# RWKV-7 recurrence with a SoLU block: decayed state made at the end of a chunk, weights narrowed in more stages, another order in the first slots

## The chip, the cores and the metric

The kernel runs on one core of one Trainium2 chip. The metric is the device time of one launch in microseconds (us), as a median over runs. The kernel before takes 893.51 us (three runs, 891.63 to 895.63). Its profiled execution has a span of 898.0 us. Times with a place in the span, such as "at 561 us", count from the start of that profiled span.

The core has five engines that work side by side, each through its own list of instructions in order: TensorE (PE; its weight loads are listed as PEld), VectorE (DVE), ScalarE (ACT), GpSimd (POOL) and SyncE (SP). SP only issues transfers here. An instruction that waits holds up all that stand behind it on its engine.

## The reference, cut to what matters

```python
for t in range(S):                       # S = 768, B = 4, H = 8, D = 40
    y[:, :, t] = einsum('bhd,bhde->bhe', rt, state)
    Sa = einsum('bhde,bhe->bhd', state, at)
    state = state * wt[:, :, None, :] - einsum('bhd,bhe->bhde', Sa, bt) + einsum('bhd,bhe->bhde', vt, kt)
x = y.transpose(0, 2, 1, 3).reshape(B * S, H * D)        # 3072 x 320
h = x @ w_in                                             # 320 x 1024
e = exp(h - max(h));  solu = h * e / (sum(e) + 1e-9)
ln = (solu - mean(solu)) / sqrt(var(solu) + 1e-6) * g_ln
out = ln @ w_out                                         # 1024 x 320
```

Thirty-two recurrences (4 batches of 8 heads), each with a 40 x 40 state, feed a row-wise block. The inputs of the recurrence are float32; `w_in`, `w_out` and `g_ln` as handed over are 64-bit or 32-bit floats, and the 64-bit weights are made into float32 on the chip.

## The kernel before, in words

Time is cut into 12 chunks (rounds) of 64 steps. A round has two **slots**, one for each half of the recurrences, so there are 24 slots, `i = 0..23`. Within a chunk the recurrence is a triangular system: its matrix is inverted once per round, and the state is carried from chunk to chunk by matmuls.

The pieces of work are Python generators, and an order written out by hand decides how they interleave on each engine:

- `front(i)` (letters f, g) makes the decayed keys of slot `i`, up to the score matrix `nt` (L276). It runs five slots ahead (`AHEAD`).
- `scatter(n)` writes the 32 x 32 blocks of `nt` of round `n` to DRAM (`blk_dram`, L385) and `gather(n)` reads them back with one matrix per partition (`blk`, L392). `gather` can be issued only when the scatter has landed.
- `invert(n)` (letter I) inverts those blocks on DVE: one start step (L400 to L404), 30 steps of a product (L410) and a subtraction (L412), and one last step that transposes (L415) and writes both forms to DRAM (L418, L420). That is 32 steps.
- `bring_inverse(i)` reads the inverse of slot `i` back in eight transfers (`tinv` L431, `tinvT` L434), and `solve(i)` (letter s) joins the blocks to 64 x 64.
- `attend(i)` (letter a) prepares what doesn't depend on the state.
- `recurrence(i)` (letter r) has six steps: the product with the state (`px` L520, added to `x` on DVE, L522); its transpose (`psT`); `pu` and its copy `nuT` on ACT (L541, L546); `plamu` and its copy `lamu` on DVE (L274, L276); `pnu`; and `pst` with the new state (L567, `tot` L573, `st` L574). `readout(i)` (letter y) makes `pyo` and the DVE copy `x` (L587, L594).
- `weights()` (letter W) fetches the weights in 26 pieces, ten of `w_in` and sixteen of `w_out` (L213), and narrows each one: DVE takes the exponent and mantissa apart (L163, L166), ACT converts them (L165, L168, L169), DVE puts the sign back (L171), POOL adds and multiplies (L173, L174). At its end the mean of the weights is taken out (L236, L238).
- `hidden(i)`, its later steps, and `output(i)` (letters h, b, o) are the row-wise block. It runs six slots behind the recurrence (`LAG`).

Ahead of slot 0 stands a prologue (fronts 0 to 3, the inverse of round 0 and eleven steps of that of round 1). Slots 0 to 5 follow the list `EARLY` and carry the weights; slots 6 to 23 follow `STEADY` and carry the row-wise block; the last six row blocks have no recurrence beside them (the tail). The lists are

```python
EARLY = ("r r f I W r a r r I W y r a f I W a s a f W a f s f W a f", ...)
STEADY = "r r f b b I r o o a o r r I o y o r I o a f h a s a h f I a h f s h f h a f h h"
```

Each `I` takes four steps. In an odd slot the first of them is the start of a new inverse, and `steps(inv, 99)` (L742) ends it at the close of the next even slot. The gather of that inverse is issued at the head of the same odd slot (L727), in the SP queue behind the scatter that the slot before issued last (L744).

Two-deep pools matter too: PSUM tiles of one bank (`bank`, two of them), of two banks (`duo`, two of them) are handed out in turn, so a copy out of PSUM that is late holds up the matmul two allocations on.

Of the kernel before, what the change touches and what calls it, by code (L numbers as in the profile page):

```python
# [9 lines left out]
FP32 = mybir.dt.float32  # L10
# [7 lines left out]
P = 128  # L18
Q = 32
# [33 lines left out]
def kernel(  # L53
# [86 lines left out]
    sm_t = zeroed(nc.vector, "sm", [P, 2, G, 64], 1)  # L140
    st_t = [const.tile([P, 2, G, D], FP32, name=f"st{i}") for i in range(2)]
# [14 lines left out]
    def narrow(dst, land, tmp):  # L156
# [8 lines left out]
        nc.scalar.activation(out=scale, in_=scale, func=AF.Relu, scale=2.0 ** 23, bias=ebias[0:n])  # L165
        nc.vector.tensor_scalar(out=man, in0=hi, scalar1=0xFFFFF, scalar2=None, op0=ALU.bitwise_and)  # L166
        frac, rest = man.bitcast(FP32), low.bitcast(FP32)
        nc.scalar.activation(out=frac, in_=man, func=AF.Copy, scale=2.0 ** -20, bias=1.0)  # L168
# [3 lines left out]
                                       op1=ALU.bitwise_or)  # L172
        nc.gpsimd.tensor_tensor(out=frac, in0=frac, in1=rest, op=ALU.add)  # L173
# [3 lines left out]
    def weights():  # L177
# [4 lines left out]
        pg = bank("pg")  # L182
        nc.tensor.transpose(out=pg[:, 0:NF], in_=g_rows, identity=ident[0:NF, 0:NF])
        nc.scalar.copy(out=g_col, in_=pg[:, 0:NF])
# [31 lines left out]
        for j in range(3):  # L216
            fetch(j)
        yield
        open_ = None
        for j, (dst, _) in enumerate(pieces):  # L220
            new = None
            if not exact:
                new = narrow(dst, land[j % 4], temps[j % 2])
            for part in (new, open_):
                if part:
                    next(part)
            open_ = new
            fetch(j + 3)
            yield
        if open_:  # L230
            next(open_)
# [78 lines left out]
    def decay(i):  # L310
# [6 lines left out]
            ax[:, :, at:at + 2].rearrange("q g c -> q c g").unsqueeze(3).to_broadcast([P, 2, G, D])  # L317
            for at in (2 * P, 2 * P + 2)]
# [6 lines left out]
        for j, n in ((1, "b"), (0, "k")):  # L325
            nc.gpsimd.tensor_tensor(out=keyed(kb[:, j])[:, :, :, 0:D], in0=by_heads(given(i, n)),  # L326
                                    in1=inv.rearrange("q (g p d) -> q p g d", p=2, d=D), op=ALU.mult)
        yield
        lo = where["cum_ex"][0]
# [17 lines left out]
    def front(i):  # L347
# [3 lines left out]
        copy = nc.scalar.copy if i < 2 else nc.gpsimd.tensor_copy  # L351
        parts = decay(i)
        next(parts)
        if i >= 2:
            copy(out=keyed(a)[:, :, :, 0:D], in_=by_heads(given(i, "a")))
# [5 lines left out]
        if i < 2:  # L361
            copy(out=keyed(a)[:, :, :, 0:D], in_=by_heads(given(i, "a")))
# [31 lines left out]
    def invert(n):  # L394
# [7 lines left out]
        nc.vector.memset(u[half(1)], 0.0)  # L402
        for p in range(2):
            nc.vector.memset(u[half(p)].rearrange("b c t -> b (c t)")[:, p:Q * Q // 2:Q + 2], 1.0)  # L404
        yield
        for j in range(1, Q - 1):
# [6 lines left out]
            yield  # L413
        ut = two.tile([P, Q, Q // 2], FP32, tag="ut", name="ut", bufs=1)
        nc.vector.tensor_copy(out=ut, in_=u.rearrange("p c t -> p t c"))  # L415
        ut_dram = of_round[n]["ut"] = dram.tile([P, Q, Q // 2], FP32, tag="ut_dram", name="ut_dram")
        u_dram = of_round[n]["u"] = dram.tile([64, Q, Q], FP32, tag="u_dram", name="u_dram")
        nc.sync.dma_start(out=ut_dram, in_=ut)  # L418
        for p in range(2):
            nc.sync.dma_start(out=u_dram.rearrange("b (c z) t -> b c z t", z=2)[:, :, p], in_=u[half(p)])  # L420
        yield

    def bring_inverse(i):
# [5 lines left out]
        for q in (0, 2):  # L429
            for p in range(2):  # L430
                nc.sync.dma_start(out=tinv[quarter(q), :, p],  # L431
                                  in_=ut[half(p)][homes(q, s)].rearrange("h s t -> s h t"))
# [75 lines left out]
    def recurrence(i):  # L508
        d = st[i]
        ci, s = divmod(i, 2)  # L510
        state, sm, nu = st_t[s], sm_t[0], nu_t[0]
        kb, vb = d["kb"], given(i, "v")
        x0 = x0_t[i % 2]
        if ci:
            nc.gpsimd.tensor_tensor(out=sm[:, :, :, 0:D], in0=state, in1=d["to_mid"], op=ALU.mult)
# [45 lines left out]
        if ci < NCH - 1:  # L561
# [9 lines left out]
            if ci:  # L571
                tot = two.tile([P, 2, G, D], FP32, tag="tot", name="tot", bufs=1)
                nc.vector.tensor_tensor(out=tot, in0=new, in1=sm[:, :, :, 0:D], op=ALU.add)  # L573
                nc.gpsimd.tensor_tensor(out=state, in0=tot, in1=d["to_end"], op=ALU.mult)  # L574
            else:
                nc.vector.tensor_tensor(out=state, in0=new, in1=d["to_end"], op=ALU.mult)
# [103 lines left out]
    def turns(order, more, **parts):  # L680

        for x in order.split():
            steps(parts.get(x), more.get(x, 1))

    def fronts(i):
# [3 lines left out]
    EARLY = ("r r f I W r a r r I W y r a f I W a s a f W a f s f W a f",  # L689
             "r r f g I W r a r r I W y r a f g I W a s a f g W a f g s f g W a f g")  # L690
    STEADY = "r r f b b I r o o a o r r I o y o r I o a f h a s a h f I a h f s h f h a f h h"
# [8 lines left out]

    with tc.manual_schedule():
        load(0, "w", "b", "a", "k")
        load(1, "w", "b")
        f, g = front(0), front(1)
        turns("f f g g f f g g f f g g f g", {}, f=f, g=g)
        scatter(0)
        load(1, "a", "k")
        gather(0)
        inv = invert(0)
        load(0, "v", "r")  # L710
        f, g, at = front(2), front(3), attend(0)
        turns("I I f f g g f f g g I f g f g I f I g a a a", dict(I=3), f=f, g=g, I=inv, a=at)
        scatter(1)
        gather(1)
        load(2, "w", "a")
        steps(inv, 99)
        bring_inverse(0)
        load(1, "v", "r")
        load(2, "b", "k")
        inv, so = invert(1), solve(0)  # L720
        turns("a a I s a I s", dict(I=4), a=at, s=so, I=inv)
        begin(0)
        ws, after, before = weights(), None, None
        for i in range(N):
            m, more, js = i - LAG, i + 1 < N, fronts(i)
            if i % 2 and (i + 3) // 2 < NCH:
                gather((i + 3) // 2)  # L727
                inv = invert((i + 3) // 2)
# [55 lines left out]
```

## Time and profile before

| stretch of the span | what runs | length, us |
|---|---|---|
| 0 to 82.9 | prologue, up to the `pu` of slot 0 | 82.9 |
| 82.9 to 302.5 | slots 0 to 5 (`pu` of slot 0 to `pu` of slot 6) | 219.6 |
| 302.5 to 361.7 | slots 6 and 7 | 59.2 |
| 361.7 to 671.0 | slots 8 to 18 | 309.3 |
| 671.0 to 773.0 | slots 19 to 22, up to the last `pu` | 102.0 |
| 773.0 to 898.0 | slot 23 and the tail | 125.0 |

Over the whole span PE is busy for 663.6 us (74%), DVE for 464.2 (52%), ACT for 272.1 (30%), POOL for 127.1 (14%). The stretches above are cut at the first `pu` matmul (L541) of a slot, since there is one per slot and it stands on the path from state to state. In the page's part 2, each digit is the busy share of a fortieth of the span (22.45 us) in tenths; PEclk is the granted TensorE clock in the same slices. In the timeline a bracket gives the idle time of the engine just before an instruction, and who ended it.

### The profile page before, as it was taken

What the parts mean: (1) busy time and instruction counts of PE and PEld (TensorE: products, weight loads), DVE (VectorE), ACT (ScalarE), POOL (GpSimd) and SP (SyncE); (2) the same over time, 40 slices, a digit from 0 to 9 for tenths busy, and PEclk for the clock granted to TensorE, in tenths of its full rate; (3) what the DMA queues carried; (4) which work ended last, traced back from release to release, by engine and by line L of the source; (5) the groups of instructions that cost most, each with busy time, mean ns of one, the idle gap of its engine ahead of it and who ended that gap; (6) DMA issues with size and microseconds to landing.
All of it is one profiled execution on the core that took longest, in us unless ns stands there. A gap on an engine that the chain in (4) does not pass through costs nothing.

```text
span 898.0 us, 28194 instructions
## 1 busy us (share of the span) xinstructions
PE 663.6 (74%) x12281; PEld 464.5 (52%) x12281; DVE 464.2 (52%) x1257; ACT 272.1 (30%) x633; POOL 127.1 (14%) x202
## 2 busy tenths in 40 slices
PE   6423726537537878989989899897988888878786
PEld 4312525426435646656656666565665665534444
DVE  2651646446443756657667675674765633222231
ACT  4110415314312332334423344233432333211111
POOL 2101304213111100111101111011100000000000
PEclk9655758657656998999999999999999999887978
DMA  6577133533533332635345453352324211000000
GB/s 111 88 129 135 38 80 84 109 76 70 100 75 55 63 64 56 97 55 95 73 82 95 74 101 77 57 104 52 58 52 79 49 28 31 8 19 7 16 15 15
DMA packets 269803, 60.01 MB, mean 67 GB/s; under 512 B 255464, under 2 KB 265328, under 8 KB 269680
## 3 DMA queue, kind: packets, MB, share of 16 engines
q1 hardware_dynamic: 269536, 57.98, 34.5%
q8 instruction: 97, 1.59, 0.8%
q10 hardware_dynamic: 144, 0.23, 0.1%
q14 instruction: 26, 0.21, 0.1%
HBM read 40.08 MB, written 13.37 MB: 60 GB/s over the span
## 4 chain that ended last, share of the span: by engine, by line
PE 51%; DVE 16%; SPq 10%; DMA 9%; ACT 7%; issue 6%; POOL 0%; ACTq 0%; DVEq 0%; POOLq 0%
PE h L615 13%; PE po L660 10%; DMA blk<-blk_dram 4%; SPq L300 4%; DVE u L412 3%; DVE prod L410 3%; PE pyo L587 3%; PE pcx L333 3%; DVE nmax L625 2%; PE pst L567 2%; DMA blk_dram<-nt 2%; SPq L385 2%; ACT e L629 2%; DVE e L632 2%; PE plnT L655 2%
## 5 line engine op out<-in xcount | busy, mean ns | idle before, releaser
L615 PE MATMUL h<-w_in,xT 128*128 128x512 f32 (+1 forms) x288 | 137.1, 682 | 19.6 <-DVE e L632 16.5
L660 PE MATMUL po<-w,lnT 128*128 128x320 f32 x384 | 129.0, 471 | 0.1
L412 DVE TENSOR_TENSOR u<-u,prod 128x30 f32<-128x30 f32 (+4 forms) x360 | 109.0, 303 | 12.4
L410 DVE TENSOR_TENSOR prod<-blk,u 128x30 f32<-128x30 f32 (+4 forms) x360 | 98.8, 274 | 10.0
L660 PEld LDWEIGHTS po<-w,lnT 128*128 128x128 f32 x384 | 71.6, 201 | 27.9 <-issue 6.8
L625 DVE TENSOR_REDUCE nmax<-h 128x1 f32<-128x1024 f32 x24 | 29.4, 1225 | 82.4 <-PE h L615 82.4
L615 PEld LDWEIGHTS h<-w_in,xT 128*128 128x128 f32 (+1 forms) x288 | 40.4, 201 | 46.3 <-issue 42.8
L665 ACT ACTIVATE osb<-po,rs 128x320 f32<-128x320 f32 x24 | 12.7, 528 | 164.1 <-PE po L660 124.0
L274 PE MATMUL plamu<-rT,nuT 64*64 64x64 f32 x768 | 18.2, 241 | 48.8 <-ACT nuT L546 48.8
L632 DVE TENSOR_TENSOR e<-h,e 128x1024 f32<-128x1024 f32 x24 | 29.4, 1225 | 44.1 <-ACT e L629 44.1
L326 POOL TENSOR_TENSOR kx<-raw_b,inv 128x320 f32<-128x320 f32 x24 | 21.0, 873 | 219.3 <-ACT inv L324 206.2
L333 PE MATMUL pcx<-cst,lw 128*128 128x132 f32 x192 | 34.6, 313 | 15.3 <-ACT y_mid L490 10.8
L333 PEld LDWEIGHTS pcx<-cst,lw 128*128 128x128 f32 x192 | 29.4, 212 | 27.0 <-ACT y_mid L490 15.9
L276 DVE TENSOR_TENSOR lamu<-plamu,cst 128x512 f32<-128x512 f32 x24 | 16.5, 689 | 50.3 <-PE plamu L274 50.3
L400 DVE TENSOR_SCALAR u<-blk 64x512 f32<-64x512 f32 x12 | 5.2, 431 | 71.9 <-DMA blk<-blk_dram 67.5
L541 PE MATMUL pu<-tinvT,x 64*64 64x64 f32 x768 | 20.2, 246 | 29.8 <-DVE x L522 19.4
L274 PEld LDWEIGHTS plamu<-rT,nuT 64*64 64x64 f32 x768 | 15.6, 153 | 50.0 <-ACT nuT L546 50.0
L647 POOL TENSOR_TENSOR rs<-c,mhalf 128x1 f32<-128x1 f32 x24 | 13.1, 548 | 194.6 <-DVE c L646 180.7
L165 ACT ACTIVATE parts<-parts,ebias 128x160 int32<-128x160 int32 (+1 forms) x26 | 11.9, 458 | 92.6 <-DVE parts L163 92.6
L656 ACT COPY lnT<-plnT 128x512 f32<-128x512 f32 x48 | 26.9, 603 | 41.7 <-PE plnT L655 41.6
L574 POOL TENSOR_TENSOR st<-tot,kx 128x320 f32<-128x320 f32 x20 | 14.8, 738 | 168.7 <-DVE tot L573 168.7
L541 PEld LDWEIGHTS pu<-tinvT,x 64*64 64x64 f32 x768 | 16.8, 150 | 39.9 <-DVE x L522 27.3
(108 smaller groups left out, 1222.4 us busy)
## 6 DMA issues: line engine op xcount, KB each, us to landing
blk<-blk_dram SPq DMA_DIRECT2D x24, 256.0 KB
raw_w<-in_w_dram SPq DMA_DIRECT2D x24, 160.0 KB
raw_b<-in_b_dram SPq DMA_DIRECT2D x24, 160.0 KB
raw_a<-in_a_dram SPq DMA_DIRECT2D x24, 160.0 KB
raw_k<-in_k_dram SPq DMA_DIRECT2D x24, 160.0 KB
v<-in_v_dram SPq DMA_DIRECT2D x24, 160.0 KB
r<-in_r_dram SPq DMA_DIRECT2D x24, 160.0 KB
out_dram<-osb SPq DMA_DIRECT2D x24, 160.0 KB
```

Source lines behind the costliest of these rows:

```text
L274: nc.tensor.matmul(t[half(c ^ p * cross), p, g * L:(g + 1) * L], lhsT=lhs[half(p), g, half(c)], rhs=rhs[half(p), g, half(c)], start=True, ...
L300: nc.sync.dma_start(out=to[half(c)], in_=ap[2 * c:2 * c + 2, :, n * L:(n + 1) * L, :] .rearrange("b h t d -> t (b h) d"))
L333: nc.tensor.matmul(t[:, g * 132:g * 132 + 132], lhsT=pair(lw, 2 * j + g), rhs=cst[:, lo:lo + 132], start=True, stop=True)
L410: nc.vector.tensor_tensor(out=t, in0=nb[:, j:j + 1, j + 1:Q].to_broadcast([P, rows, m]), in1=u[:, 0:rows, j:j + 1].to_broadcast([P, rows, ...
L412: nc.vector.tensor_tensor(out=u[:, 0:rows, j + 1:Q], in0=u[:, 0:rows, j + 1:Q], in1=t, op=ALU.subtract)
L541: nc.tensor.matmul(t[half(z), c ^ p, h // 2 * L:h // 2 * L + L], lhsT=x0[half(c ^ p), h, :], rhs=d["tinvT"][half(c ^ p), p, h % G, :], sta ...
L587: nc.tensor.matmul(t[half(p), c, g * L:g * L + L], lhsT=kb[half(c), j, 2 * g + p, :], rhs=lam[half(c), h % 2, h // 2, :], start=i < 2 and ...
L615: nc.tensor.matmul(h[:, j * 512:j * 512 + 512], lhsT=of_round[i // 2]["xT"][rows, kt, i % 2 * P:i % 2 * P + P], rhs=w_in[rows, 4 if kt == ...
L625: nc.vector.tensor_reduce(out=nmax, in_=h, axis=AX.X, op=ALU.max, negate=True)
L632: nc.vector.tensor_tensor(out=q, in0=h, in1=e, op=ALU.mult)
L656: nc.scalar.copy(out=lnT[:, fs.start:fs.stop].rearrange("p f t -> p (f t)"), in_=t)
L660: nc.tensor.matmul(o[:, 0:DM], lhsT=lnT[:, f, :], rhs=w2[:, f, :], start=f == 0, stop=f == NF - 1)
```

## The change

**Decayed state.** The kernel before ends a chunk with `state = tot * to_end` and begins the next with `sm = state * to_mid`, both on POOL. The changed kernel forms the small factor `fac = to_end * to_mid(next)` (128 x 8) and ends the chunk with `sm = tot * fac`; `sm` is kept for both slots of a round and `st` is dropped.

**Weights in stages.** A piece is narrowed in four steps instead of two: DVE apart, ACT, DVE sign, POOL, each in a half-step `W` of its own; there are ten `W` in a slot in place of five, and pieces are fetched two ahead instead of three. `g_rows` is transposed at the end of the weights, no longer at their start.

**Order of the first slots.** The prologue loads in another order, doesn't interleave the inverse of round 0 (it runs as one block), leaves that of round 1 to slot 0, and brings the first `tinv` by the ACT queue. The `a` copies are all on POOL, and `k` is multiplied a step after `b`.

**Inverses as one stream.** All later inverses are one generator. In `EARLY` and `STEADY` the first `I` of a slot now stands behind `lamu` (the fourth r), not ahead of `pu`. The steps per `I` are `[6, 6, 3, 3]` in an even slot and `[0, 6, 4, 4]` in an odd one, so that a new inverse starts behind the sixth r of an odd slot. Half of the start of an inverse (a memset of 64 x 512 and one of 64 x 16) moves to POOL. `kT` moves ahead of `pu`, the front's `pcum` behind it, and the second half of the `plnT` transposes behind `plamu`; `b` and `k` are loaded in mid-slot.

```diff
-    sm_t = zeroed(nc.vector, "sm", [P, 2, G, 64], 1)
-    st_t = [const.tile([P, 2, G, D], FP32, name=f"st{i}") for i in range(2)]
+    sm_t = zeroed(nc.vector, "sm", [P, 2, G, 64], 2)
...
-        pg = bank("pg")
-        nc.tensor.transpose(out=pg[:, 0:NF], in_=g_rows, identity=ident[0:NF, 0:NF])
-        nc.scalar.copy(out=g_col, in_=pg[:, 0:NF])
...
-            new = None
-            if not exact:
-                new = narrow(dst, land[j % 4], temps[j % 2])
-            for part in (new, open_):
-                if part:
-                    next(part)
+            new = None if exact else narrow(dst, land[j % 4], temps[j % 2])
+            for _ in range(2):
+                for part in (open_, new):
+                    if part:
+                        next(part)
+                if _:
+                    fetch(j + 2)
+                yield
             open_ = new
-            fetch(j + 3)
-            yield
...
-        nc.vector.memset(u[half(1)], 0.0)
-        for p in range(2):
-            nc.vector.memset(u[half(p)].rearrange("b c t -> b (c t)")[:, p:Q * Q // 2:Q + 2], 1.0)
+        nc.gpsimd.memset(u[half(1)], 0.0)
+        for p, engine in enumerate((nc.vector, nc.gpsimd)):
+            engine.memset(u[half(p)].rearrange("b c t -> b (c t)")[:, p:Q * Q // 2:Q + 2], 1.0)
...
+        if ci < NCH - 1:
+            fac = small.tile([P, 2, G], FP32, tag="fac", name="fac")
+            nc.gpsimd.tensor_tensor(out=fac, in0=d["to_end"], in1=st[i + 2]["to_mid"], op=ALU.mult)
+            factor = fac.unsqueeze(3).to_broadcast([P, 2, G, D])
         if ci:
-            nc.gpsimd.tensor_tensor(out=sm[:, :, :, 0:D], in0=state, in1=d["to_mid"], op=ALU.mult)
...
-                nc.gpsimd.tensor_tensor(out=state, in0=tot, in1=d["to_end"], op=ALU.mult)
+                nc.gpsimd.tensor_tensor(out=sm[:, :, :, 0:D], in0=tot, in1=factor, op=ALU.mult)
...
-    EARLY = ("r r f I W r a r r I W y r a f I W a s a f W a f s f W a f",
-             "r r f g I W r a r r I W y r a f g I W a s a f g W a f g s f g W a f g")
-    STEADY = "r r f b b I r o o a o r r I o y o r I o a f h a s a h f I a h f s h f h a f h h"
+    EARLY = ("r r a r f r W I r W y W r I W W a f L a s W a f W a W I f I W s f W a f",
+             "r r a r f g r W I r W y W r I W W a f g L a s W a f g W a W I f g I W s f g W a f g")
+    STEADY = "r r b b a r f o r o I o r o y o r I o a f L h a s a h f a I h f I s h f h a f h h"
...
+    def inverse_steps(i):
+        if i < 3:
+            return [[6, 6, 6, 6], [0, 3, 4, 3], [6, 6, 5, 5]][i]
+        return [0, 6, 4, 4] if i % 2 else [6, 6, 3, 3]
...
-        load(1, "w", "b")
...
-        inv = invert(0)
         load(0, "v", "r")
-        f, g, at = front(2), front(3), attend(0)
-        turns("I I f f g g f f g g I f g f g I f I g a a a", dict(I=3), f=f, g=g, I=inv, a=at)
+        load(1, "k")
+        f, g, at, inv, so = front(2), front(3), attend(0), invert(0), solve(0)
+        turns("f g f g f f g g", {}, f=f, g=g)
+        load(2, "w", "a", "b", "k")
+        turns("a a I", dict(I=99), a=at, I=inv)
+        bring_inverse(0, nc.scalar)
+        turns("a a a f g f g a f g", {}, f=f, g=g, a=at)
         scatter(1)
         gather(1)
...
             if i % 2 and (i + 3) // 2 < NCH:
                 gather((i + 3) // 2)
-                inv = invert((i + 3) // 2)
+            if i == 1:
+                steps(inv, 8)
...
             if i % 2 == 0:
-                load((i + 6) // 2, "w", "a", "b", "k")
-            turns(EARLY[len(js) - 1] if i < LAG else STEADY, dict(I=4), **parts)
+                load((i + 6) // 2, "w", "a")
+                parts["L"] = later((i + 6) // 2)
+            turns(EARLY[len(js) - 1] if i < LAG else STEADY, dict(I=inverse_steps(i)), **parts)
...
-            else:
-                steps(inv, 99)
```

## The prediction

> **What bounds the kernel now.** I cut the span at the `pu` matmul (L541) that stands once in each slot: 82.94, 107.48, 148.68, 186.37, 219.67, 256.79, 302.55 us for slots 0 to 6, then 326.84, 361.73, 388.80, 419.48, 445.86, 475.19, 501.56, 529.77, 556.14, 586.53, 612.89, 644.60, 670.98. The view of busy time by stretch comes first (us of the stretch, then busy time of PE, PEld, DVE, ACT, POOL, then the granted clock, the DMA share and GB/s):
>
> ```profile
> 0.00:82.90 82.90, 29.12 (x377) 22.17 (x377) 33.22 (x112) 16.07 (x35) 15.06 (x30) 0.70 0.70 117
> 82.90:302.50 219.60, 125.51 (x2881) 103.26 (x2881) 110.82 (x331) 70.40 (x190) 48.04 (x77) 0.68 0.37 75
> ...
> 361.70:671.00 309.30, 276.76 (x5742) 191.78 (x5742) 200.33 (x533) 111.62 (x252) 44.69 (x65) 0.98 0.42 77
> ```
>
> For 302 us no engine is near full and PE runs at two thirds of its clock: latency bounds. Slots 8 to 18 are PE's, 276.8 of 309.3 us. Next, who waited for whom (us, times, longest):
>
> ```profile
> ACT parts L165 <- DVE parts L163: 92.6, 18, 19.6
> ...
> DVE u L400 <- DMA blk<-blk_dram: 67.5, 11, 10.3
> ...
> PE plamu L274 <- ACT nuT L546: 48.8, 5, 20.4
> ...
> PE pyo L587 <- DVE lamu L276: 22.4, 8, 5.1
> ...
> PE pg L183 <- DMA g_rows<-in_moe_g_ln_dram: 16.7, 1, 16.7
> ```
>
> These are links of one chain, as the timeline of slot 1 shows:
>
> ```profile
> 121.04 1.13 SPq L392 DMA_DIRECT2D blk<-blk_dram  x2
> ...
> 124.65 0.42 DVE L400 TENSOR_SCALAR u<-blk 64x512 f32<-64x512 f32 x1 [9.17 <-DMA blk<-blk_dram]
> ...
> 127.73 0.51 ACT L165 ACTIVATE parts<-parts,ebias 128x256 int32<-128x256 int32 x1 [19.65 <-DVE parts L163]
> ...
> 128.77 0.70 ACT L546 ACTIVATE nuT<-pu 128x256 f32<-128x256 f32 x3
> 129.18 0.94 PEld L274 LDWEIGHTS plamu<-rT,nuT 64*64 64x64 f32 x32 [20.61 <-ACT nuT L546]
> 129.18 1.13 PE L274 MATMUL plamu<-rT,nuT 64*64 64x64 f32 x32 [20.37 <-ACT nuT L546]
> ```
>
> DVE waits for the gather, ACT for DVE's L163 behind it, and `nuT` stands behind that on ACT. Slots 3 and 5 repeat it (10.6 us each). In the late odd slots only DVE's part is left (slot 15):
>
> ```profile
> 561.49 0.42 DVE L400 TENSOR_SCALAR u<-blk 64x512 f32<-64x512 f32 x1 [3.38 <-DMA blk<-blk_dram]
> ...
> 564.17 0.68 DVE L276 TENSOR_TENSOR lamu<-plamu,cst 128x512 f32<-128x512 f32 x1
> ```
> ```profile
> 564.91 0.69 PE L587 MATMUL pyo<-lamu,kx 64*64 64x64 f32 x32 [2.29 <-DVE lamu L276]
> ...
> 566.23 2.35 PE L660 MATMUL po<-w,lnT 128*128 128x320 f32 x4
> ```
>
> The gap in front of `pyo` is followed by `po` at 2.35 us where the even slot before has 1.34: the gap is paid about twice.
>
> **What the skill says.** The Trainium skill's "TensorE: Matmul & The Clock Gate", Part 1, says that the array falls to half rate after an idle window of about 3.4 us and needs as long a busy one to recover. The trace agrees in kind: `plamu` of 32 takes 1.13 us after a stall and 0.65 in a full slot. Its "DMA: Bandwidth & Descriptors", "Anatomy of one DMA", says that [...]waits on semaphores are taken by the issuing sequencer. The trace: the gather is issued 1.9 us behind the scatter's last issue in slots 14 and 15, and SP does nothing else meanwhile. Its "Trainium Kernel Development and Optimization", "Key Constraints", says that another issuing queue saves only issue time. Four `tinv` issues take 1.8 to 2.2 us here, so moving them to ACT is worth no more.
>
> **Part by part.**
>
> *Steady slots.* Even slots last 26.37 us (slots 10 to 18; slot 8 27.07). Odd ones with a gather last 30.68, 29.33, 28.21, 30.39, 31.71 (slots 9 to 17): excess over 26.37 is 4.3, 3.0, 1.8, 4.0, 5.3, sum 18.4. The start of an inverse moves behind `tot`, some 9 us later than now (561.5 against 570.9), when `blk` has been there for 9 us. So the wait goes, and its cold clock. Slot 19 has no front, and lasts 27.3 us where slot 21, with no gather either, takes 25.4: 1.9 more. Slot 7 lasts 34.9 us with a 5.1 us wait for `lamu` and cold matmuls; without them it is like slot 6, 24.3 us: 10. Order on PE: `kT` now fills the gap ahead of `pu` (0.41 + 0.49 us idle, because `x` L522 comes late), `pcum` no longer waits for L319, and `po` no longer for both `lnT`: 0.3 us in each of some 15 slots, 4.5. Added: six inverse steps behind `lamu` of an even slot take 6 x 0.63 = 3.8 us instead of 2.5. `x` L594 stands behind them and `pst` needs the PSUM pair that `x` frees. But `plnT`'s half, `po`, `pnu`, `po`, `pyo`, which lie between, are 5.2 us of PE: hidden. On POOL half the start of an inverse (0.5 us, as the DVE memset) stands behind `sm`; L412 waits for it 1 us, and only `psi` is behind, needed 8 us later. The decayed state: 22 POOL multiplications of 0.74 us go, 22 of 128 x 8 come. `st` was ready at 541.4 and `sm` needed at 553: worth nothing. Sum: 18.4 + 1.9 + 10 + 4.5 = 34.8 us.
>
> *Prologue.* Now `tinvT` is done at 63.0 and `pu` starts at 82.94, since `pg` waits for `g_rows` in front of it. That wait goes. The uninterrupted inverse: 60 operations with gaps, 16.9 us, plus 0.9, from 27 (two loads fewer ahead of the gather, now 28.7) to 45. Then `u` and `ut` issues 1.7, landing 3.5, `tinv` on ACT 2, `rT` 0.6 (it stands behind them on ACT), then PE from `plamv` to `pz` about 9.5, `tinvT` 0.9: `pu` at 63, 20 us earlier.
>
> *Slots 0 to 5.* That gain is not kept, because SP's queue is as long as before. The last `nt` of round 1 comes at about 60. Behind it on SP: scatter 2.3, its landing 1.9, gather 1.1, `v` and `r` 2.8, eight returns 4.0, `w` and `a` 2.8, `g_rows` 0.7: the first weight piece is issued at 75.8 and lands at 79.5 (3.7 us from issue to the DVE that waits for it at 174.78). In slot 0 DVE's L163 for it stands ahead of `x`, and `pst` behind `x`: `pst` at 81 (now 88.8). Then six inverse steps and a piece stand ahead of `vT` (ACT waits for the piece: 7 us), and twelve steps around `paT`: the `pu` of slot 1 comes at 107, as now. Slot 1 loses its 20.4 us stall, but DVE begins with eight steps (4.3 us). The seventh piece is queued on SP behind scatter, gather, the writes of `u` and `ut`, 3.5 us of landing and eight returns: issued at 122, landed at 126, with DVE and ACT waiting from 119. `pu` of slot 2 at 142 (now 148.7): 6.7 us won. Slots 2 and 4: now 37.7 and 37.1, of which 7.5 + 4.5 and 6.5 + 3.9 are waits for pieces and for the ending inverse; the pieces come in time, as `b` and `k` are loaded behind them. But six steps and a piece between `pst` and `vT` cost some 4.5: 30.2 and 31.2, 7.5 and 5.9 won. Slot 3, 33.3, loses 10.6; the gather now holds DVE at `tot` for about 1 us and the piece behind it for 1.5, with three more for steps: 28.2, 5.1 won. Slot 5, 45.8, likewise loses 10.6 and some 2.2 of half-rate matmuls behind the stall: 33, 12.8 won. `mean` itself (7.1 us and 4 us of waiting) stays. Sum 0 + 6.7 + 7.5 + 5.1 + 5.9 + 12.8 = 38.0.
>
> The tail has no change. Total 38.0 + 34.8 = 72.8: 893.5 - 72.8 = 820.7 us.
>
> **Unknown costs, both ends.** How long SP holds a piece back in slots 0 and 1: nothing (all of the prologue's 20 us and the 20.4 us stall won, some 34 more than my 6.7) or another 8 us in each of slots 1, 3, 5. I take the queue as counted, since every issue in it has a row now. How many of the moved steps show on the path in slots 2 to 5: none (3 to 4.5 us less each) or all six plus cold clock (3 us more each).
>
> **The rivals.** *All stalls go, and none takes their place:* slots 0 to 5 then run at the 24.5 us that slot 0 takes now, plus 12 for `mean`: 159 from 63 on, so `pu` of slot 6 at 222, 80 won; with 34.8, 778 us. For it: DVE has 110.8 us to do in 219.6. Against: SP's issues alone, some 40 us per two slots, stand in order with those two landings. Chance 0.10. *The start gives nothing:* the pieces, fetched two ahead instead of three, wait for SP in every slot and take back the 38. Then 859 us. For it: DVE waited 9.7 us twice for pieces fetched three ahead. Chance 0.15. *Slower:* blocks of six steps hold up `x`, `psi`, `paT`'s copy; PE, which is 89% busy in the steady part, goes cold in each slot, 1.3 us of wait paid twice in 17 slots is 44, and the steady gain is eaten; the start loses 20 to piece waits. 893.5 - 34.8 + 44 + 20 = 923 us. Against: DVE is busy for 18.0 of the 26.4 us of slot 14, so 8 us are free. Chance 0.04.
>
> **How the numbers follow.** The forecast has 0.71: 820.7 us. Its own bounds are 800 (half the missed start) and 840 (three slots with 8 us more, less the rest). The range of 796 to 850 takes in these, half of the case in which the start gives nothing and a little of the best. Faster 0.95 (all but the last case and its fringe), the same 0.01, slower 0.04.
>
> **What would show it.** In the changed profile: `pu` of slot 0 near 63 and of slot 6 near 264; no wait of DVE L400 longer than 1 us from slot 7 on; steady odd slots as long as even ones, 26.2 us; PE waits in slots 0 and 1 that end on DVE, behind transfers named `bits`. It would be wrong if `pu` of slot 6 stays near 300, or if steady slots wait for `x` behind inverse steps.

## The result and the profile after

The changed kernel takes 850.08 us (846.64 to 853.63) where the kernel before took 893.31 beside it: ratio 0.9515, interval 0.9466 to 0.9563. The forecast was 820.7 us. So the direction was right, and 43 us came where 73 were forecast; the measured time lies at the upper end of the forecast's range of 796 to 850 us. The profiled pair differs by more, 898.0 against 844.7 us: the profiled run of the changed kernel is the fastest of its four timed ones, and that of the kernel before took longer than all of its timed ones. About 4.5 us of that pair's difference lie behind the last `pu` (at 772.2 us in the kernel before, not at 773.0 as in the table of the time before), in 440 matmuls whose granted clock differed (0.83 against 0.85). The list of the tail is the same in both kernels, and the profiles of the changed kernel and of those variants of it that keep this tail have 121.3 to 124.7 us behind the last `pu`; so most of the 4.5 us can be chance.

The start of `pu` (L544 now), in us, for slots 0 to 8 and 19: 66.70, 116.54, 151.25, 180.45, 209.81, 238.49, 276.08, 297.90, 325.11 and 627.25. Cut there, forecast and measurement stand like this:

| stretch | gain forecast | gain in the profiles |
|---|---|---|
| start to `pu` of slot 0 | 20.0 | 16.2 |
| slot 0 | -20.0 | -25.3 |
| slots 1 to 5 | 38.0 | 35.5 |
| slots 6 and 7 | 10.6 | 10.2 |
| slots 8 to 18 | 21.7 | 7.1 |
| slot 19 to the end | 2.5 | 9.5 |
| sum | 72.8 | 53.2 |

(The forecast's 0.3 us per slot for the order on PE is spread over the slots 6 to 20.) The view of busy time by stretch, of the changed kernel, with the columns as in the prediction:

```profile
66.70:276.10 209.40, 122.40 (x2886) 101.36 (x2885) 116.84 (x352) 72.19 (x192) 53.60 (x90) 0.72 0.47 94
...
325.10:599.90 274.80, 251.10 (x5223) 179.72 (x5223) 175.67 (x476) 102.47 (x230) 39.12 (x70) 0.96 0.44 83
```

The slots 0 to 5 are still latency: PE has no more to do than before and runs at 0.72 of its clock. In the steady slots 8 to 17 the granted clock is 0.96, lower than before, although the long stalls are gone. The list of waits says what took their place:

```profile
PE pu L544 <- DVE x L525: 25.5, 13, 2.7
...
PE pcx L337 <- ACT vT L259: 22.8, 2, 22.1
...
DVE parts L162 <- DMA bits<-in_moe_w_in_dram: 18.2, 2, 11.3
DVE prod L410 <- POOL u L404: 17.5, 8, 8.9
...
DVE u L400 <- DMA blk<-blk_dram: 14.3, 4, 8.1
...
PE py L478 <- DMA bits<-in_moe_w_in_dram: 10.0, 1, 10.0
```

(`pcx`, `paT` and `pbT` belong to a front, `vT` and `psi` to `attend`, `py` and `pz` to `solve`; `plnT` are the transposes of the row-wise block that stand ahead of `po`, its last product.)

DVE's wait for the gather fell from 67.5 us in eleven places to 14.3 in four, and PE no longer waits for `nuT` or `pg`. Two of the new lines are not in the forecast's sum: DVE waits for GpSimd's memset, 8.9 us once, and PE waits for `x` in front of `pu` thirteen times, 1.36 us at the end of even slots and 2.67 at the end of odd ones, where it had waited 0.49. The timeline of the prologue shows the first:

```profile
24.44 0.42 DVE L400 TENSOR_SCALAR u<-blk 64x512 f32<-64x512 f32 x1 [8.06 <-DMA blk<-blk_dram]
...
25.90 2.02 SPq L302 DMA_DIRECT2D raw_k<-in_k_dram  x2
...
31.41 1.67 POOL L327 TENSOR_TENSOR kx<-raw_k,inv 128x320 f32<-128x320 f32 x2 [12.06 <-DMA raw_k<-in_k_dram]
...
33.14 0.52 POOL L402 MEMSET u<- 64x512 f32 x1
...
33.87 0.19 DVE L410 TENSOR_TENSOR prod<-blk,u 128x30 f32<-128x30 f32 x1 [8.87 <-POOL u L404]
```

The change issues the second round's `k` only behind the first gather, at 25.90. GpSimd's multiplications of `k` wait for it, and the memset of half of `u`, now on GpSimd too, stands behind them. DVE, whose part was done at 25.0, starts the inverse at 33.9. The second is seen at the end of slot 15 (an odd one; PE's and DVE's lines in one order of time):

```profile
540.83 0.29 DVE L412 TENSOR_TENSOR u<-u,prod 128x126 f32<-128x126 f32 x1
540.84 0.68 PE L523 MATMUL px<-sm,kx 64*64 64x40 f32 x32
541.04 1.22 DVE L628 TENSOR_REDUCE nmax<-h 128x1 f32<-128x1024 f32 x1
...
542.17 0.68 DVE L278 TENSOR_TENSOR nt<-pnt,cst 128x512 f32<-128x512 f32 x1
543.53 1.23 DVE L635 TENSOR_TENSOR e<-h,e 128x1024 f32<-128x1024 f32 x1 [0.67 <-ACT e L632]
544.67 0.48 DVE L525 TENSOR_TENSOR x<-x_own,px 128x320 f32<-128x320 f32 x1
545.20 0.75 PE L544 MATMUL pu<-tinvT,x 64*64 64x64 f32 x32 [2.67 <-DVE x L525]
...
546.74 1.06 PE L658 MATMUL plnT<-cst,e 128*128 128x128 f32 x4
```

`h` was done at 539.7, but the last group of inverse steps holds DVE until 541.0. So `nmax` (the row maximum of `h`), then the exponential on ACT, then `q` (their product, the line with `e<-h,e`) are late, and `x`, whose `px` was ready at 541.5, stands behind `q`. PE idles 2.67 us, and `plnT` then runs at 1.06 us where it takes 0.60 at full rate.

### The profile page after: what moved, and what is told of

Same layout as the page of the kernel before. It is cut to its first block, busy times and chain, and to the rows that moved or that the text cites. A ratio compares the mean times of both kernels' runs of the same rounds, so it can differ in the third digit from the quotient of the medians.

```text
span 844.7 us, 28254 instructions
## 1 busy us (share of the span) xinstructions
PE 646.6 (77%) x12281; PEld 462.1 (55%) x12281; DVE 451.1 (53%) x1234; ACT 272.3 (32%) x631; POOL 126.3 (15%) x228
## 4 chain that ended last, share of the span: by engine, by line
PE 59%; DVE 14%; SPq 8%; DMA 6%; issue 6%; ACT 5%; POOL 0%; ACTq 0%; DVEq 0%; POOLq 0%
PE h L618 13%; PE po L663 13%; PE plnT L658 4%; DVE u L412 3%; DVE prod L410 3%; PE pcx L337 3%; DVE e L635 3%; PE pyo L590 2%; SPq L302 2%; PE py L478 2%; PE pst L570 2%; PE pu L544 2%; PE plamv L276 2%; PE pyo L504 2%; DVE nmax L628 2%
## 5 line engine op out<-in xcount | busy, mean ns | idle before, releaser
L663 PE MATMUL po<-w,lnT 128*128 128x320 f32 x384 | 120.4, 446 | 0.0
L410 DVE TENSOR_TENSOR prod<-blk,u 128x30 f32<-128x30 f32 (+4 forms) x360 | 98.8, 274 | 29.5 <-POOL u L404 17.5
L412 DVE TENSOR_TENSOR u<-u,prod 128x30 f32<-128x30 f32 (+4 forms) x360 | 102.2, 284 | 12.4
L663 PEld LDWEIGHTS po<-w,lnT 128*128 128x128 f32 x384 | 69.2, 194 | 24.3 <-issue 3.5
L618 PEld LDWEIGHTS h<-w_in,xT 128*128 128x128 f32 (+1 forms) x288 | 40.1, 201 | 45.8 <-issue 42.3
L544 PE MATMUL pu<-tinvT,x 64*64 64x64 f32 x768 | 21.0, 250 | 36.4 <-DVE x L525 25.5
L278 DVE TENSOR_TENSOR lamv<-plamv,cst 128x512 f32<-128x512 f32 x24 | 16.6, 692 | 56.5 <-PE plamv L276 56.5
L478 PE MATMUL py<-tinv,nt 32*32 32x32 f32 x768 | 19.8, 204 | 29.2 <-ACT vT L259 19.2
L544 PEld LDWEIGHTS pu<-tinvT,x 64*64 64x64 f32 x768 | 17.4, 155 | 42.5 <-DVE x L525 29.7
L658 PE MATMUL plnT<-cst,e 128*128 128x128 f32 x192 | 38.1, 342 | 3.2 <-DVE e L635 3.2
L597 DVE TENSOR_TENSOR x<-pyo,kx 128x512 f32<-128x512 f32 x24 | 16.6, 690 | 43.2 <-PE pyo L590 42.9
L276 PE MATMUL plamv<-rT,vT 64*64 64x64 f32 x768 | 19.1, 246 | 26.7 <-ACT rT L259 26.4
L658 PEld LDWEIGHTS plnT<-cst,e 128*128 128x128 f32 x192 | 29.0, 177 | 14.7 <-issue 10.7
```

The costliest lines, as they stand in the source:

```text
L276: nc.tensor.matmul(t[half(c ^ p * cross), p, g * L:(g + 1) * L], lhsT=lhs[half(p), g, half(c)], rhs=rhs[half(p), g, half(c)], start=True, ...
L278: nc.vector.tensor_tensor(out=dst, in0=t[:, :, 0:G * L].rearrange("q p (g c) -> q p g c", g=G), in1=tri.unsqueeze(1).unsqueeze(1).to_broad ...
L410: nc.vector.tensor_tensor(out=t, in0=nb[:, j:j + 1, j + 1:Q].to_broadcast([P, rows, m]), in1=u[:, 0:rows, j:j + 1].to_broadcast([P, rows, ...
L412: nc.vector.tensor_tensor(out=u[:, 0:rows, j + 1:Q], in0=u[:, 0:rows, j + 1:Q], in1=t, op=ALU.subtract)
L478: nc.tensor.matmul(t[quarter(out), c:c + Q], lhsT=lhs(p, g), rhs=rhs(p, g), start=True, stop=True)
L544: nc.tensor.matmul(t[half(z), c ^ p, h // 2 * L:h // 2 * L + L], lhsT=x0[half(c ^ p), h, :], rhs=d["tinvT"][half(c ^ p), p, h % G, :], sta ...
```

## The experiments

Ratios are against the kernel before; the changed kernel's is 0.9515, and 0.001 is 0.9 us. They are told by the term of the forecast that they test. Profiles of kernels with the same prologue put `pu` of slot 0 between 66.7 and 68.3 us, so a difference of a microsecond or two in one stretch of one profile says little.

**The prologue's memset: on which engine.**

```diff
-        nc.gpsimd.memset(u[half(1)], 0.0)
-        for p, engine in enumerate((nc.vector, nc.gpsimd)):
-            engine.memset(...)
+        nc.vector.memset(u[half(1)], 0.0)
+        for p in range(2):
+            nc.vector.memset(...)
```

> The changed kernel with both memsets of the inverse's start back on DVE, nothing else. Theory A (in the prologue GpSimd's half stands behind its multiplications of k, which wait for a late load, and holds the inverse 8.9 us): L410 starts near 25.6 instead of 33.87, the inverse ends near 42.6, pu of slot 0 comes near 58 to 60, the first weight piece is issued about 8 us earlier, and the total falls by 6 to 10 us, to 840 to 844. In the steady slots DVE does 0.52 us more and waits 1.2 us less, eight times: at most 1 us in the total. Rival B (pu of slot 0 waits for the second round's fronts and for SP's queue anyway): the inverse ends earlier but pu of slot 0 and the first weight piece stay within 2 us, total 848 to 852.

Ratio 0.9366 (0.9319 to 0.9413). `pu` of slot 0 comes at 59.5 instead of 66.7, `pu` of slot 6 at 269.0 instead of 276.1, and from slot 6 on the slots are as long as with the memset on GpSimd. The first weight piece is now taken up at 80.72:

```profile
80.72 0.29 DVE L162 TENSOR_SCALAR parts<-bits 128x256 int32<-128x256 int32 x1 [11.22 <-DMA bits<-in_moe_w_in_dram]
```

So theory A holds: the 7.2 us of the prologue are kept until the end. (By the ratios the gain is 13 us, by the profiled spans 7.3. The trace places 7.1 of these in front of slot 6, and the intervals of the ratios are 4 us wide on each side.)

**The same wait, by the load in front of it.** Here the memset stays on GpSimd and the `k` that its predecessors wait for is fetched early. (The kernel before issues it between the first scatter and the gather, not ahead of the scatter as the expectation says.)

```diff
-        load(1, "b")
+        load(1, "b", "k")
...
         load(0, "v", "r")
-        load(1, "k")
```

> The changed kernel with the second round's k loaded beside its b, ahead of the first scatter, as the kernel before has it; the memsets stay on GpSimd. Theory A (the memset is late only since the multiplications of k ahead of it on GpSimd wait for that late load): L410 starts at 27 to 29 instead of 33.9 (the scatter and gather come up to 2 us later behind two more issues), pu of slot 0 near 60 to 63, total 4 to 7 us less, ratio 0.943 to 0.948. Rival B (the memset on GpSimd is late by itself, or the two issues delay the gather as much as the wait was): L410 and pu of slot 0 within 2 us of now, ratio 0.949 to 0.954.

Ratio 0.9410 (0.9349 to 0.9471). GpSimd has its memsets done before DVE has the gather:

```profile
19.83 1.68 POOL L327 TENSOR_TENSOR kx<-raw_k,inv 128x320 f32<-128x320 f32 x2 [0.77 <-DMA raw_k<-in_k_dram]
21.57 0.52 POOL L402 MEMSET u<- 64x512 f32 x1
```

L410 starts at 26.13, `pu` of slot 0 at 58.9, both a little earlier than theory A's ranges. The two more issues ahead of the scatter delay L400 by 0.4 us only. So the memset on GpSimd is harmless when `k` is early, and the late `k` is harmless when the memset is on DVE: two edits of the change, each harmless alone, met in one queue. By slot 6 the gain is down to 4.5 us, since slots 1 and 5 are 1.3 and 1.1 us longer; why was not looked into.

**The fourth group of inverse steps.**

```diff
-        return [0, 6, 4, 4] if i % 2 else [6, 6, 3, 3]
+        return [0, 8, 6, 0] if i % 2 else [6, 6, 3, 3]
```

> The changed kernel with the odd steady slots' fourth group of inverse steps (4 steps, some 2.4 us of DVE just ahead of nmax) moved into the second and third: 0, 8, 6, 0 instead of 0, 6, 4, 4. Theory A (these steps make nmax, and with it e, q and x, late in odd slots): nmax starts when h is done, the wait of pu for x at the end of an odd slot falls from 2.66 to about 1.3 us, plnT and plamu are at full rate behind it, odd slots take 26 to 26.5 us instead of 27.3; over seven such slots 5 to 9 us, total 841 to 845. Rival B (x is late because it stands behind q on DVE whatever is ahead of nmax, or eight steps hold psi and x_own up instead): slots stay at 27.0 to 27.5, total 848 to 852. Rival C (the steps behind tot hold psi and lamv, so that PE waits there): 853 to 860.

Ratio 0.9365 (0.9314 to 0.9417). From slot 8 on odd slots take 26.3 us and even ones 25.9, instead of 27.3 and 27.4; slots 8 to 18 together 286.8 us instead of 302.1. Busy time by stretch, slots 12 and 13 of this kernel:

```profile
433.90:459.80 25.90, 24.24 (x526) 17.34 (x526) 18.99 (x52) 10.25 (x23) 3.59 (x6) 1.00 0.54 98
459.80:486.00 26.20, 24.25 (x522) 17.28 (x522) 16.19 (x45) 10.22 (x23) 4.22 (x8) 1.00 0.42 79
```

PE's 24.2 us are its work at full clock; in the changed kernel it is busy for 25.7 us of the even slots 12 and 14 at a granted clock of 0.94. So of the 2.5 us won per pair of slots, 1.0 is the wait at the end of the odd slot (1.65 us instead of 2.66) and 1.5 is the cold clock that the even slot behind it no longer has. The edit also reached slots 3 and 5, where the moved steps did harm: slot 5 took 42.3 us instead of 37.6. `pu` of slot 6 came 5.7 us later; 2.1 of these were there at the `pu` of slot 3, up to which nothing was edited.

**The place of `x` on DVE.** The steps stay; `x` of the next slot is queued ahead of `q` instead of behind it.

```diff
-    STEADY = "r r b b a r f o r o I ... h f h a f h h"
+    STEADY = "r b r b b a r f o r o I ... h f h a f h"
...
-            turns("h h o o h h b b h o o o o h h", {}, h=now, b=after, o=before)
+            turns("b h h o o h h b b h o o o o h h", {}, h=now, b=after, o=before)
```

> The changed kernel with the state part's x (L525) queued on DVE ahead of q (L635) of the slot before instead of behind it; the inverse's steps stay as they are. Theory A (pu waits because x stands behind q, which waits for e on ACT): x follows nt at once, the 1.36 us wait in front of pu at the end of even slots and the 2.66 us at the end of odd ones fall to under 0.5, with the half-rate matmuls behind them; slots take 25 to 26 us instead of 27.3, over 16 slots 20 to 35 us, total 815 to 830. Rival B (PE only meets the same wait at plnT, which needs q): pu is early but plnT waits 1 to 2 us; slots 26.5 to 27.3, total 838 to 850.

Ratio 0.9068 (0.9027 to 0.9108), the largest gain of any single edit: 40 us by the ratios, 37.5 us in the profiles between the `pu` of slot 6 and that of slot 23. DVE's timeline at the end of slot 14 and PE's line behind it show `x` no longer behind `q`:

```profile
498.83 0.49 DVE L525 TENSOR_TENSOR x<-x_own,px 128x320 f32<-128x320 f32 x1
499.39 1.23 DVE L635 TENSOR_TENSOR e<-h,e 128x1024 f32<-128x1024 f32 x1
499.64 0.75 PE L544 MATMUL pu<-tinvT,x 64*64 64x64 f32 x32
```

Slots take 25.4 and 24.8 us. The expected wait at `plnT` (rival B) does not come: `pu` and `pcum` give `q` the 1.2 us that it needs. The list of waits in front of PE has 6.2 us for `x` instead of 25.5. Theory A holds for both this run and the one before: the steps made the wait longer, the order on DVE made it.

**The steady slots alone.** The kernel before, with only the new order, steps and loads from slot 6 on.

```diff
-    STEADY = "r r f b b I r o o a o r r I o y o r I o a f h a s a h f I a h f s h f h a f h h"
+    STEADY = "r r b b a r f o r o I o r o y o r I o a f L h a s a h f a I h f I s h f h a f h h"
...
-            turns(... STEADY, dict(I=4), **parts)
+            turns(... STEADY, dict(I=4 if i < LAG else
+                  [0, 6, 4, 4] if i % 2 else [6, 6, 3, 3]), **parts)
```

> The kernel before with the new order of the steady slots alone (from slot 6 on: the new order, the inverse begun behind tot in odd slots with 6, 4, 4 steps and continued with 6, 6, 3, 3 in even ones, b and k loaded later); prologue, slots 0 to 5, weight pieces, state and memsets as before. Theory A (the gain of the steady part doesn't need the start's): slots from 8 on 27.0 to 27.6 us, odd as even, with a wait of 2 to 3 us for x in front of pu; the total 20 to 30 us less, ratio 0.966 to 0.978. Rival B (the steady gain needs memsets on GpSimd or the new state): less than 12 us, ratio above 0.987. Rival C (as predicted, 26.2 us slots): 33 to 38 us, ratio 0.957 to 0.963.

Ratio 0.9805 (0.9770 to 0.9840), 17 us: less than theory A's 20 to 30, more than rival B's 12. The lengths are theory A's, 27.3 and 27.4, and the wait is there:

```profile
PE pu L541 <- DVE x L522: 33.8, 16, 3.7
```

So the 27.3 us belong to the new order, steps and loads of these slots; they need neither the changed start nor the memsets on GpSimd nor the new state. The forecast's 26.2 (rival C) is excluded.

**The decayed state alone**, on the kernel before.

```diff
-            nc.gpsimd.tensor_tensor(out=sm[...], in0=state, in1=d["to_mid"], op=ALU.mult)
+            nc.gpsimd.tensor_tensor(out=fac, in0=d["to_end"], in1=st[i + 2]["to_mid"], op=ALU.mult)
...
-                nc.gpsimd.tensor_tensor(out=state, in0=tot, in1=d["to_end"], op=ALU.mult)
+                nc.gpsimd.tensor_tensor(out=sm[...], in0=tot, in1=factor, op=ALU.mult)
```

> The kernel before with the decayed state alone (two sm tiles, fac on GpSimd, no st). Theory A (as predicted: st was ready some 11 us ahead of sm, and GpSimd had room): no change, ratio 0.995 to 1.005 and slots of the same lengths. Rival B (px waited for sm at the start of slots, hidden behind other waits): ratio 0.985 to 0.994. Rival C (fac waits for the front of the slot after next, and holds px): above 1.005.

Ratio 1.0016 (0.9998 to 1.0034). It is worth nothing, as forecast.

**The transpose of `g_rows` alone**, on the kernel before.

```diff
         nc.sync.dma_start(out=g_rows, in_=moe_g_ln.rearrange("(c p) -> c p", p=P))
-        pg = bank("pg")
-        nc.tensor.transpose(out=pg[:, 0:NF], in_=g_rows, identity=ident[0:NF, 0:NF])
-        nc.scalar.copy(out=g_col, in_=pg[:, 0:NF])
...
+        pg = bank("pg")
+        nc.tensor.transpose(out=pg[:, 0:NF], in_=g_rows, identity=ident[0:NF, 0:NF])
+        nc.scalar.copy(out=g_col, in_=pg[:, 0:NF])
         gb = two.tile([P, NF, P], FP32, tag="e", name="gb", bufs=1)
```

> The kernel before with the transpose of g_rows (pg) and its copy moved behind the last weight piece, nothing else. Theory A (as predicted: pu of slot 0 comes some 16 to 20 us earlier, but SP's queue in front of the first piece and the gather is as long as before, and takes it back): pu of slot 0 near 64 to 67, pu of slot 1 at 103 to 108 (107.5 before), ratio 0.994 to 1.002. Rival B (what is won in front of pu stays won): pu of slot 1 at 85 to 92, ratio 0.975 to 0.985.

Ratio 0.9954 (0.9939 to 0.9969). `pu` of slot 0 comes at 66.0 instead of 82.9, and `pu` of slot 1 at 101.4 instead of 107.5. Of 16.9 us won in front of slot 0, 6.1 are left one slot later, and 4.4 by the timed runs. This is theory A, with a little more left than it said. The timelines of SP and PE, in one order of time, show who takes it back:

```profile
65.99 1.00 PE L541 MATMUL pu<-tinvT,x 64*64 64x64 f32 x32
...
81.15 16.29 SPq L210 DMA_DIRECT2D bits<-in_moe_w_in_dram  x10
86.74 1.25 PE L333 MATMUL pcx<-cst,lw 128*128 128x132 f32 x4 [14.52 <-ACT vT L257]
```

The first piece is issued at 81.15, in the kernel before at 80.15: SP has the loads and returns to issue first, and that queue doesn't depend on when `pu` comes.

**The weight pieces in another queue.**

```diff
-                nc.sync.dma_start(out=to[row:row + part.shape[0]], in_=part)
+                nc.scalar.dma_start(out=to[row:row + part.shape[0]], in_=part)
```

> The changed kernel with the transfers of the weight pieces issued by ACT instead of SP. Theory A (pieces are late in slots 0 and 1 because they stand behind the scatter, gather, loads and returns in SP's queue): DVE's waits for bits of 11.3 and 7.0 us and PE's of 10.0 us fall to under 2; pu of slot 1 comes 10 to 14 us earlier, pu of slot 6 15 to 20, total 830 to 836. Rival B (ACT's own queue is as blocked, and some 60 issues at 0.45 us each, 4.5 us in a slot, make it late): gain under 5 us, total 845 to 855, with longer waits for nuT and vT.

Ratio 0.9313 (0.9272 to 0.9354). `pu` of slot 1 comes at 109.3 instead of 116.5, and `pu` of slot 6 at 264.3 instead of 276.1: 11.8 us, between the theories' bounds and nearer to A. (By the ratios the gain is 18 us.) No wait for `bits` is left on DVE or PE. The first piece is issued at 70.3 instead of 84.6: in the changed kernel the issues of other transfers fill some 14 of the 15 us of SP's time between the start of the gather's issue and the piece. Slot 0 lost 8.4 us, less than the 11.3 us of the wait for `bits`, since DVE now waits longer for the gather, which stands ahead of the piece in its queue and lands later (L400 starts at 76.82 instead of 73.12; why was not looked into):

```profile
76.82 0.42 DVE L400 TENSOR_SCALAR u<-blk 64x512 f32<-64x512 f32 x1 [5.24 <-DMA blk<-blk_dram]
...
81.46 0.29 DVE L162 TENSOR_SCALAR parts<-bits 128x256 int32<-128x256 int32 x1
```

**Slot 5.** The changed kernel's slot 5 lost 8.2 us, not the forecast's 12.8.

```diff
+        if i == LAG - 1:
+            return [0, 0, 7, 7]
         return [0, 6, 4, 4] if i % 2 else [6, 6, 3, 3]
```

> The changed kernel with slot 5's fourteen inverse steps moved from the second, third and fourth group (0, 6, 4, 4) into the last two (0, 0, 7, 7). Theory A (the last weight piece's L171 stands behind six steps on DVE, so gb and mean are 3.5 us late): the wait of mean for gb falls from 6.7 to 3 to 3.5 us, slot 5 from 37.6 to 34 to 35 us, total 3 us less, ratio 0.945 to 0.951. Rival B (the steps now hold the copy of paT, and pz waits that much longer): mean 3.5 us earlier, but slot 5 stays within 1 us of 37.6, ratio 0.950 to 0.955.

Ratio 0.9442 (0.9404 to 0.9480). Slot 5 takes 32.2 us, even below theory A's 34. The timelines of PE, first of the changed kernel, then of this one:

```profile
251.02 7.10 PE L238 MATMUL mean<-w,gb 128*128 128x320 f32 x16 [6.68 <-ACT gb L235]
...
268.86 0.69 PE L478 MATMUL pz<-tinvT,y_mid 32*32 32x32 f32 x32 [3.48 <-DVE kx L368]
```
```profile
247.03 4.57 PE L238 MATMUL mean<-w,gb 128*128 128x320 f32 x16 [2.84 <-ACT gb L235]
...
263.56 1.06 PE L478 MATMUL pz<-tinvT,y_mid 32*32 32x32 f32 x32 [4.69 <-DVE kx L368]
```

The wait fell by 3.8 us, as expected: in the changed kernel the last piece's L171 stands behind six inverse steps on DVE, and `gb` behind L171. Some of it comes back: the moved steps now hold the copy of `paT` (L368), and `pz` waits 1.2 us longer, as rival B said, but less than the 3.8 us. The 2.5 us by which `mean` itself is shorter are its clock, and they are luck, as the combined run below shows.

**Slot 0.** `vT` ahead of the first piece on ACT, and the inverse's steps 10, 8, 3, 3.

```diff
-             "r r a r f g r W I r W y W r I W W a f g L a s W ..."
+             "r r a r f g r W I r W a y W r I W W f g L a s W ..."
...
-            return [[6, 6, 6, 6], [0, 3, 4, 3], [6, 6, 5, 5]][i]
+            return [[10, 8, 3, 3], [0, 3, 4, 3], [6, 6, 5, 5]][i]
```

> The changed kernel with slot 0's order mended: vT is copied on ACT ahead of the first piece's narrowing, and the inverse's steps are 10, 8, 3, 3 instead of 6, 6, 6, 6. Theory A (PE's 22 us in front of pcx are vT standing on ACT behind a piece, and pz's 6.1 us are steps ahead of the copy of paT): slot 0 falls from 49.8 to 38 to 42 us, pu of slot 1 comes 8 to 12 us earlier; as the second slot then waits for the pieces the longer, pu of slot 6 comes 3 to 10 earlier, ratio 0.940 to 0.948. Rival B (pcx and paT only wait for the next thing, the fronts' loads b and k and psi behind the piece): pu of slot 1 less than 4 us earlier, ratio 0.948 to 0.953.

Ratio 0.9483 (0.9439 to 0.9526), `pu` of slot 1 at 115.3: 1.2 us earlier. The ratio lies where theory A's range ends and rival B's begins; the trace is rival B's. PE's 22.1 us in front of `pcx` are gone, and in their place stands

```profile
PE ppsi L276 <- DVE x L597: 19.3, 3, 16.2
```

that is `x`, which DVE does behind the first piece, as before. The piece's arrival is the bound of slot 0; `vT` was only the first to show it.

**Three edits together:** memsets on DVE, pieces issued by ACT, `x` ahead of `q`, each as above.

> The changed kernel with the three edits that each helped alone: memsets on DVE, weight pieces issued by ACT, x ahead of q. Theory A (they act in different stretches: 7 us in the prologue, 12 in slots 0 and 1, 37 from slot 6 on, by the pu of the three runs alone): total 790 to 798, pu of slot 6 near 257, steady slots 25.1. Rival B (the first two share a stretch, since with pieces in time slot 0 waits for the gather of the next inverse instead): pu of slot 6 at 262 to 268, total 799 to 806.

Ratio 0.8909 (0.8861 to 0.8957), 793.4 us, `pu` of slot 6 at 257.3: 18.8 us earlier, where the first two alone gave 7.1 and 11.8. This is theory A: the edits act in different stretches and add up.

**All of them:** those three, slot 0's order, slot 5's steps, and the steps 0, 8, 6, 0 in odd slots from 7 on.

> The changed kernel with the three edits of the combined run before (memsets on DVE, pieces issued by ACT, x ahead of q) and three more: the order of slot 0, the steps of slot 5, and from slot 7 on no steps in the fourth group of odd slots. Theory A (each takes away a wait that the combined run still shows: some 8 us in slot 0, 3 in slot 5, 0.6 in each of eight slots): 776 to 784 us against the 793 of the combined run, pu of slot 1 at 92 to 95. Rival B (the waits move: slot 1 waits for its pieces, PE, busy for 24.2 of the 25.1 us of a steady slot, has no more to give): 787 to 793.

Ratio 0.8743 (0.8701 to 0.8786), 781.1 us, the fastest version here. The total is theory A's, the reasons are so only in part. Slots 8 to 18 took 270.8 us in the profile instead of 276.8, and the profiled span fell by 6.8 us, less than the medians did (12.3). Slot 0 stayed at 41 us, with `pu` of slot 1 at 101.7 and not at the expected 92 to 95. Slot 5 stayed at 37.6, though its wait for `gb` is as short as in the run of slot 5 (6.57 us with three edits):

```profile
228.27 7.39 PE L238 MATMUL mean<-w,gb 128*128 128x320 f32 x16 [2.84 <-ACT gb L235]
...
249.44 1.07 PE L478 MATMUL pz<-tinvT,y_mid 32*32 32x32 f32 x32 [5.08 <-DVE kx L368]
```

What was won in front of `mean` went elsewhere in the slot: `mean` ran at half rate, as with three edits (7.16 us), `pz` waited 5.08 us for the copy of `paT` behind the moved steps instead of 3.48, and the matmuls from the second `pcx` (1.25 us instead of 0.72) to `pz` ran at half rate too. In this kernel the other place of slot 5's steps is worth nothing.

## Why the forecast was right, and where it was too high

- *Start and slot 0: the mechanism was right, one term was missing.* The wait for `g_rows` went, the inverse ran without breaks, and SP's queue took the gain back at the first piece (`bits`), as foretold; that queue is shown by the pieces' move to ACT and by the transpose alone. What failed is the step "half the start of an inverse (0.5 us, as the DVE memset) stands behind `sm`; L412 waits for it 1 us, and only `psi` is behind". It priced the memset by its place in the steady slots (there the wait is 1.2 us, on L410) and didn't look at what stands ahead of it on GpSimd in the prologue. The step "two loads fewer ahead of the gather" saw that `k` (two transfers) is loaded later and counted only the gain. The two together cost 7 to 8 us. With the memset undone, `pu` of slot 0 comes at 59.5 (forecast 63), the first piece is taken up at 80.7 (forecast 79.5), `pu` of slot 1 comes at 109.2 (107) and of slot 2 at 144.6 (142).
- *Slots 1 to 5: right in sum, by misses that cancel in part.* 35.5 of 38.0 us. The 48.8 us for which PE waited for `nuT` are gone, as foretold. Which edit removed them (the narrowing in four steps, the later start of an inverse, the new order) is not shown: none of these was tried alone in the first slots. Slot by slot the gains were 6.5, 8.5, 3.9, 8.4 and 8.2 where 6.7, 7.5, 5.1, 5.9 and 12.8 were forecast. Slot 5 failed at "`mean` itself (7.1 us and 4 us of waiting) stays": the wait grew to 6.7, because six inverse steps were put ahead of the last piece (the run of slot 5 took 3.8 us off it), and the wait of `pz` for the copy of `paT` behind other steps grew from 0.85 to 3.48. The two runs that moved these steps show that they lengthen one wait or the other.
- *Slots 6 and 7: right in sum only, which is luck:* 10.2 of 10.6 us. Slot 7 gained 7.7 us, where 10.3 were forecast, and slot 6 gained 2.5, where 0.3 were.
- *Slots 8 to 18: the largest miss, 14.6 us.* The waits for the gather went as foretold, and odd slots became like even ones. But they became 27.3 us and not 26.2 (26.1 by the forecast's own sum). The step that failed is "`kT` now fills the gap ahead of `pu`", with "0.3 us in each of some 15 slots" for the order on PE: the gap grew to 1.36 and 2.67 us. The step looked at PE's queue and not at the one that feeds it: the inverse's steps were moved to just ahead of `nmax`, and `x` stands behind `q`, as it did in the kernel before. The six steps behind `lamu`, which the forecast did examine, were hidden. With the fourth group moved, these slots gain 22.5 us, near the 21.7 forecast, and with `x` ahead of `q` 33.1. The prediction's own sign of being wrong, "steady slots wait for `x` behind inverse steps", is what came.
- *Decayed state:* nothing, as forecast. The move of `tinv` to ACT and the order of the prologue were not tried alone.
- *Slot 19 to the end:* 9.5 us where 2.5 were forecast. Some 4.5 of them are the clock of the last stretch, most of it perhaps chance; the rest was not looked into.
- *The rivals.* "Slower" named the right place (steps that hold `x` back, PE cold in each slot) and 44 us for it; it came at about a third. The case in which the start gives nothing didn't come: the start gave 26.5 us.

What is common to the misses of the prologue and of the steady slots is told by the Trainium skill's "Perfetto Trace Analysis", in the note under "Tensor Engine Instruction (MATMUL, LD_WEIGHTS)": ACT, DVE and GpSimd are strict first-in-first-out. The traces agree: a memset of 0.52 us that needed nothing held DVE up for 8.9 us, and an addition of 0.48 us with its inputs ready stood 3 us behind `nmax`, `nt` and `q`.

## What to carry to other kernels

When an instruction is moved to another engine, read that engine's queue at every place where the moved line occurs, the prologue's single occurrence first, and ask which transfer its predecessors wait for. When PE idles in front of a matmul, look at what stands ahead of its operand on the engine that makes it: moving one short addition ahead of one that waited for ACT gave some 40 us here, almost as much as the whole change. And when one queue issues everything, a gain ahead of it is kept only if what it must issue next comes earlier too: with the transpose alone the first piece was issued at 81.2 instead of 80.2 us and two thirds of the gain went, with the memset on DVE it was issued at 76.9 instead of 84.6 and all of the gain stayed.

## What the runs showed of the hardware

In these runs the clock of a stretch could not be foretold from the gap in front of it. The same 16 matmuls took 4.57 us in one kernel and 7.39 in another behind the same idle time of 2.84 us. Behind 2.67 us of idle time the first four `plnT` of a steady slot took 0.90 to 1.06 us; behind 1.36 us, and behind 1.66 in the run of the fourth group, they took 0.60. The Trainium skill's "TensorE: Matmul & The Clock Gate", Part 1, says that the activity window of about 3.4 us is free-running, and that the point at which the rate changes therefore depends on where in the window the first matmul lands; these runs agree with it, but do not show the window itself. An idle gap as long as the window, which the prediction took from there, was not needed for the fall to half rate: 2.67 us were enough. For a forecast it means that a gap of 2 to 3 us in front of a long row of matmuls has to be costed with both rates: here 2.8 us of difference, as much as the gap.
